# Moving the attention into the first product, and splitting one more half-size product a second time

## The chip, the cores and the metric

The kernel runs on one core of one Trainium2 chip. The metric is device microseconds (us) of one execution; the kernel before takes 954.35 us, the median of three runs that lie between 954.01 and 954.46 us. Everything is 32-bit float.

Engines are named as the profile names them: PE is TensorE, PEld its weight loads, DVE is VectorE, ACT is ScalarE, SPq is the queue of SyncE, from which nearly all transfers are issued.

## The reference

```python
# attention without softmax: batch 8, 8 heads, 576 positions, head size 64
kv  = np.einsum('bhsd,bhse->bhde', k, v)
out = np.einsum('bhsd,bhde->bhse', q, kv)
rms = np.sqrt(np.mean(out * out, axis=-1, keepdims=True) + 1e-06)
x   = (out / rms * g_norm)         # then laid out as 4608 tokens x 512
# feed-forward part, d_model 512, d_ff 2048
h = x @ w_in
r = np.maximum(h, 0.0)
g = s * (r * r) + b
y = g @ w_out
```

## The kernel before: the parts that the change touches

The 4608 tokens are taken in nine units (u = 0 to 8) of 512 tokens. A unit has two stages. The first stage (`mm1`) makes h and g, in four steps s = 0 to 3 of 512 columns of h each. The second stage (`mm2`) makes y. Beside these, the attention of a unit is made in four chunks of 128 tokens; each chunk has four parts: `turn` (DVE transposes q), `product` (16 small matmuls on PE, a square on ACT, a sum on DVE), `norm` (a root on ACT, a reciprocal and a multiply on DVE), and `turn_x` (DVE transposes the result, ACT scales it).

Both large products use a Strassen-Winograd scheme: a 2 x 2 block product is made of seven products of sums of blocks in place of eight. They are numbered 1 to 7 here; the sums on the token side are called S1 to S4, those on the weight side T1 to T4. In the second stage product 5 is S1 T1, product 6 is S2 T2, product 7 is S3 T3, and product 3 has S4. From unit 2 on, products 1, 2, 7 and 4 of the second stage are themselves made by the same scheme ("twice"): seven products of 128 x 128 blocks. A plain product of the seven is 2 x 8 matmuls of 128x256 (`product`, once for each half j of 256 tokens); one made twice is 7 x 4 matmuls of 128x128 (`second_level`, `go`).

```python
TWICE = (1, 2, 7, 4)
ORDER = (1, 2, 6, 7, 5, 3, 4)

def product(i, j, ps, first):          # a plain product, one half j: 8 matmuls of 128x256
    for f in range(FC // 2):
        s, b = divmod(f, 2)
        ...
        matmul(ps, ga[G_OF[i], s][:, b, j * P : j * P + P], w2, first and f == 0, f == FC // 2 - 1)

def scaled(o, ps, other):              # DVE: o = ps * s + other   (line 671 of the profile)
    nc.vector.scalar_tensor_tensor(o, ps, s_col, other, ALU.mult, ALU.add)

def second_level(i, other, to, x_tag="y"):
    def sums(which=(5, 6, 7, 3)):      # four DVE adds or subtractions of 128x512 (lines 230, 233)
        ...
    def go(m, bank, first):            # 4 matmuls of 128x128
        ...
    def keep(name, j, q):
        r[name] = late["tmp"].tile([P, P], FP32, name="r", tag="r")
        scaled(r[name], t["x"], other(j, cols[q]))
    def m1():
        go(1, "x", True)
        keep("r1", 0, 0)               # r1 is read out of bank x ...
    def m2():
        go(2, "z", True)
        scaled(to(0, cols[0]), t["z"], r["r1"])
    def m6():
        go(6, "x", False)              # ... before product 6 is accumulated onto bank x
        keep("r2", 1, 0)
    ...                                # m7 on bank y, m5 and m3 on x, m4 on y
```

So each product made twice asks for four sums ahead (128x512), and for seven small reads of PSUM (128x128). Product m6 adds to the bank that m1 left, and may start only when DVE has read r1 out of it.

The second stage in its order, with the attention of the next unit in between:

```python
            ...                        # product 1 twice; the last of the first stage lies in it
            product_q[0]()             # attention, chunk 0
            p2[1]()
            step["x3_s3"]()
            p2[2](); p2[6]()
            s2((0, 1))
            p2[7](); p2[5]()
            s2((2, 3))
            pump(2)
            norm[0]()
            p7["sums"]()
            x6_of(0)
            p2[3](); p2[4]()
            ...                        # two adds of b_12
            attend(1); turn_x[0](); turn[2]()
            x6_of(1)
            p7[1]()
            s4((0,))
            p7[2](); p7[6]()
            ...                        # attend(2), x5_of(0), p7[3], p7[4], attend(3), x5_of(1), x3, p4
```

(Calls that stood on lines of their own are set side by side here, and `pump` calls are cut in places.) DVE carries out its instructions in this order of the program.

Weights of the second stage come through a ring of seven buffers of 4 KB per partition; `pump(n)` issues the next n loads of a queue, each of which waits on SPq until its buffer is free. k and v have two buffers of their own; q is loaded at the start of a unit for the next one.

```python
late["ring"] = ctx.enter_context(tc.tile_pool(name="ringp", bufs=7, side="right"))
late["sub"]  = ctx.enter_context(tc.tile_pool(name="subp", bufs=5, side="right"))
late["kv"]   = ctx.enter_context(tc.tile_pool(name="kvp", bufs=2, side="right"))
```

Of the kernel before, what the change touches and what calls it, by code (L numbers as in the profile page):

```python
# [16 lines left out]
def kernel(  # L17
# [78 lines left out]
    def load_kv(b, i, pool, queues=(nc.sync, nc.sync), **kw):  # L96

        t = pool.tile([P, 4 * R * D], U32, name="kv_sb", **kw)
        kv_in[b, i] = t.bitcast(FP32).rearrange("p (m l j d) -> p m l j d", m=2, l=2, j=R)
        for m, src in enumerate((k, v)):  # L100
            for r, queue in enumerate(queues):
                h = NP * r + 2 * i
                queue.dma_start(  # L103
                    out=kv_in[b, i][r * HB : r * HB + HB, m].rearrange("p l j d -> p l (j d)"),
                    in_=src[b, h : h + 2].rearrange("h (p j) d -> p h (j d)", j=R),
                )
# [168 lines left out]
    TWICE = (1, 2, 7, 4)  # L275
# [55 lines left out]
    b_12 = const.tile([P, HN], FP32, name="b_12")  # L331

    def bias_row():

        nc.vector.tensor_scalar(out=b_sq, in0=b_sq, scalar1=b_col, scalar2=None, op0=ALU.mult)
        ps = ps_t.tile([P, DM], FP32, name="b_ps", tag="t")
        matmul(ps, b_sq, b_row, True, True)
        nc.scalar.copy(b_row, ps)
        sub(b_12, b_row[:, :HN], b_row[:, HN:])
# [8 lines left out]
    def kv_product(b):  # L348


        ps = [ps_t.tile([P, 2, D], FP32, name="kv_ps", tag="t") for _ in range(2)]
        for i in range(2):
            if b == 0:
                warm((18, 7)[i])
            kv = kv_in.pop((b, i))
            for j in range(R):
                for l in range(2):
                    for r in range(2):
                        rows = slice(r * HB, r * HB + HB)
                        nc.tensor.matmul(  # L360
                            ps[r][l * HB : l * HB + HB, i, :],
                            lhsT=kv[rows, 0, l, j, :],
                            rhs=kv[rows, 1, l, j, :],
                            start=(j == 0),
                            stop=(j == R - 1),
                        )
        for r in range(2):
            for l in range(2):
                ls = slice(l * HB, l * HB + HB)
                to = bd_kv[b % 2][ls, 2 * r : 2 * r + 2, ls].rearrange("p i (c e) -> p i c e", c=KC)  # L370
                src = ps[r][ls].rearrange("p i (e c) -> p i c e", c=KC)
                if b == 0 and l == 1:
                    nc.vector.tensor_copy(out=to, in_=src)
                else:
                    nc.scalar.copy(to, src)

    xT = {}

    def attention(c, first=False):
# [70 lines left out]
        def turn_x():  # L450
            u, j = divmod(c, 4)
            if j == 0:
                xT[u] = xp.tile([P, KC, 2 * TB], FP32, name="xT", tag="xT")
# [175 lines left out]
    late = {}  # L629

    def twice(u, i):
        return u > 1 and i in TWICE

    queue_w2 = [
        (u, i, n) for u in range(1, U) for i in ORDER for n in range(4 if twice(u, i) else 2)
    ]

    def pump(k):

        for u, i, n in queue_w2[:k]:  # L640
            t = late["ring"].tile([P, 4 * HN], FP32, name="w2_sb", tag="w2")
# [14 lines left out]
    def mm2(u, step=None, att=None):  # L656


# [30 lines left out]
        def second_level(i, other, to, x_tag="y"):  # L689
# [23 lines left out]
            def go(m, bank, first):  # L713
                if first:
                    tag = {"x": x_tag}.get(bank, bank)
                    t[bank] = bank_of((bank, i), tag, 1 if tag == "z" else 2)
                    t[bank] = t[bank].rearrange("p b n -> p (b n)")[:, :P]
# [119 lines left out]
        def x3(j):  # L837
            product(3, j, st["x", j], False)
            scaled(rows("o1", j)[:, HN:], st["x", j], b2 if u == 1 else st["o1", j][:, HN:])
# [44 lines left out]
        if u == 1:  # L884
# [5 lines left out]
                lambda: x6(0),  # L890
# [11 lines left out]
        def right(name, j, q=slice(0, HN)):  # L902
            return rows(name, j)[:, HN:][:, q]

        p1 = second_level(1, lambda j, q: b2[:, q], lambda j, q: right("o1", j, q), "x")
        p2 = second_level(2, lambda j, q: right("o1", j, q), lambda j, q: rows("o1", j)[:, q])
        p7 = second_level(
            7, lambda j, q: right("o1", j, q), lambda j, q: right("o2", j, q)
        )
        p4 = second_level(4, lambda j, q: st["r2", j][:, q], lambda j, q: rows("o2", j)[:, q])  # L910

        def x6_of(j):
            st["x", j] = half(("x", j), "x")
            product(6, j, st["x", j], True)
            part("r2", j, st["x", j], b_12)

        def x5_of(j):
            product(5, j, st["x", j], False)

        def with_7(j):  # L920

            to = right("o2", j)
            add(st["r2", j], st["r2", j], to)
            scaled(to, st["x", j], to)
# [10 lines left out]
        turn, product_q, norm, turn_x, x_sums_next = att or [[lambda: None] * 4] * 5  # L935

        def attend(c):
            product_q[c]()
            norm[c]()

        def sums_ahead():
            p1["sums"]()
            turn[0]()
            turn[1]()

        def all_of_it():
# [12 lines left out]
            p1[4]()  # L959
            step["x3_s1"]()  # L960
            pump(2)
            product_q[0]()
            p2[1]()
            step["x3_s3"]()
            p2[2]()
            p2[6]()
            s2((0, 1))
            p2[7]()
            p2[5]()
            s2((2, 3))  # L970
            pump(2)
            norm[0]()
            p7["sums"]()
            x6_of(0)
            p2[3]()
            p2[4]()
            for j in range(2):
                left = rows("o1", j)[:, :HN]
                add(left, left, b_12)
            pump(2)  # L980
            attend(1)
            turn_x[0]()
            turn[2]()
            x6_of(1)
            pump(2)
            p7[1]()
            s4((0,))
            p7[2]()
            p7[6]()
            s4((1,))  # L990
            p7[7]()
            s4((2,))
            p7[5]()
            s4((3,))
            pump(2)
            attend(2)
            turn_x[1]()
            turn[3]()
            x5_of(0)
            p7[3]()  # L1000
            with_7(0)
            p7[4]()
            pump(2)
            attend(3)
            turn_x[2]()
            x5_of(1)
            with_7(1)
            turn_x[3]()
            pump(2)
            p4["sums"]()  # L1010
            x3(0)
            for m in (1, 2, 6, 7, 5):
                p4[m]()
            pump(2)
            x_sums_next[0]()
            x3(1)
            pump(2)
# [4 lines left out]
        return sums_ahead, all_of_it  # L1022
# [4 lines left out]
    def tc_late():  # L1027
        convp.release()
        late["ring"] = ctx.enter_context(tc.tile_pool(name="ringp", bufs=7, side="right"))
        late["sub"] = ctx.enter_context(tc.tile_pool(name="subp", bufs=5, side="right"))  # L1030
        late["tmp"] = ctx.enter_context(tc.tile_pool(name="tmpp", bufs=4, side="right"))
        late["kv"] = ctx.enter_context(tc.tile_pool(name="kvp", bufs=2, side="right"))
# [93 lines left out]

    def side_of(u):

        if u + 1 >= U:
            return None  # L1130
        turn, product, norm, turn_x, _ = zip(*(attention(c) for c in range(4 * u + 4, 4 * u + 8)))
        if u > 1:
            sums = lambda: [sums() for sums in x_sums(u + 1)]
            return turn, product, norm, turn_x, [sums]
# [25 lines left out]

    kv_due = {(b // 2 * R + b % 2 * 4) // 4 - 1: b for b in range(2, B)}

    def loads(u):
        if u + 1 < U:
            load_q(4 * u + 4)
            load_q(4 * u + 6)
# [14 lines left out]

    for u in range(U):
        if u > 0:
            loads(u)
        steps = [mm1(u, s) for s in range(NS)] if u > 0 else []

        def x3(a):
            for name in ("x3", "x3_square", "x3_s1", "x3_s3"):  # L1190
                a[name]()

        def y4(a):
            for name in ("y4", "y4_square"):
                a[name]()

        slots = []
        for s, a in enumerate(steps):
            slots.append(a["x1"])
            if s:  # L1200
                slots.append(partial(x3, steps[s - 1]))
            slots.append(a["z2"])
            if s:
                slots.append(partial(y4, steps[s - 1]))
            slots += [a["x6"], a["y7"], a["x5"]]
        if u == 0:
            first_unit()
        side = side_of(u)
        second = mm2(u, steps[-1], side) if u > 1 else mm2(u)
        for n, slot in enumerate(slots):  # L1210
            slot()
            if u > 1 and n == len(slots) - 2:
                second[0]()
            if u == 1 and n in (1, 3, 5):
                for sums in sums_w_in((n + 1) // 2):
                    sums()
            if u in kv_due and n == 12:
                kv_product(kv_due[u])
            elif u + 1 in kv_due and n == 14:
                for i in range(2):  # L1220
                    load_kv(kv_due[u + 1], i, late["kv"], tag="kv")
        if u > 1:
            second[1]()
            continue
        for n, slot in enumerate(second):
            slot()
            if u == 0:
                if n == 1:
# [3 lines left out]
                    loads(0)  # L1232
# [13 lines left out]
        if u == 0:  # L1246
            tc_late()
            for i in range(2):
                load_kv(kv_due[1], i, late["kv"], tag="kv")
# [31 lines left out]
```

## Time and profile before

| | busy us | share of the span | instructions |
|---|---|---|---|
| span | 954.8 | | 17222 |
| PE | 939.9 | 98% | 7102 |
| DVE | 611.3 | 64% | 1100 |
| ACT | 194.5 | 20% | 366 |

Line 91 is the helper that issues every matmul but those of the attention (line 422) and of k times v (line 360). Lines 230 and 233 are the DVE helpers `add` and `sub`, line 671 is `scaled`, line 569 the copy of a partial result by ACT in the first stage. Lines 155 and 103 load q, and k and v; 645 and 648 are the ring's loads, 772 the stores. The names before and after the arrow are of tiles: `x_ps`, `y_ps`, `z_ps` and `t_ps` are PSUM banks, `sub` are sums, `r` is what `keep` leaves, `o` are rows of the output, `qT` and `xT` the turned q and x.

In the chain of waits a count such as x16 holds both the matmuls and their weight loads: x16 is eight matmuls.

### The profile page before, as it was taken

Reading aid. Unit: us, or ns where it says so; the run is one execution under the profiler, and the core shown is the slowest. Engines: PE = TensorE matmul, PEld = TensorE weight load, DVE = VectorE, ACT = ScalarE, POOL = GpSimd, SP = SyncE. Lnnn points to the kernel's source line nnn. Section 1 sums busy time; section 2 is a strip of 40 time slices with the busy share of each in tenths; the row PEclk is TensorE's granted clock in tenths of the full one; section 3 lists DMA queues with packets and bytes.
Section 4 is the critical chain, followed back from the end, with each engine's and each line's share of the span. In section 5 each row is a group of like instructions: output and inputs, shape, how many; then the busy total and the mean of one; then the engine's idle time right before and its main releaser. Section 6 shows DMA issues by size and latency. Waiting matters only on the chain.

```text
span 954.8 us, 17222 instructions
## 1 busy us (share of the span) xinstructions
PE 939.9 (98%) x7102; PEld 839.9 (88%) x7102; DVE 611.3 (64%) x1100; ACT 194.5 (20%) x366; POOL 6.7 (1%) x18
## 2 busy tenths in 40 slices
PE   6999999999999999999999999999999999999997
PEld 6888888888889998999889988989899989998997
DVE  1779768475447854686368744884478557864673
ACT  2674132211111112111211212121211111111100
POOL 2000000000000000000000000000000000000000
PEclk9999999999999999999999999999999999999999
DMA  9588929587735666365437554566225541662063
GB/s 216 192 310 230 309 69 260 107 249 253 210 69 140 181 189 138 76 201 159 128 81 200 185 159 84 159 197 181 32 81 180 184 87 42 202 176 68 20 223 100
DMA packets 131709, 151.09 MB, mean 158 GB/s; under 512 B 76592, under 2 KB 89136, under 8 KB 131504
## 3 DMA queue, kind: packets, MB, share of 16 engines
q1 hardware_dynamic: 128528, 148.22, 54.1%
q10 hardware_dynamic: 2784, 1.77, 0.8%
q8 instruction: 56, 0.92, 0.4%
q14 instruction: 21, 0.17, 0.1%
q0 software_dynamic: 320, 0.00, 0.0%
HBM read 125.83 MB, written 24.12 MB: 157 GB/s over the span
## 4 chain that ended last, share of the span: by engine, by line
PE 95%; DMA 2%; DVE 1%; ACT 1%; issue 0%; SPq 0%; ACTq 0%; DVEq 0%
PE x_ps L91 49%; PE y_ps L91 32%; PE z_ps L91 9%; PE x_ps L422 3%; PE kv_ps L360 2%; DMA w_raw<-in_moe_w_in_dram 1%; DMA kv_sb<-in_k_dram 1%; PE qT_ps L401 0%; DVE xn L441 0%; DVE xT L465 0%; ACT xT L471 0%; ACT w_raw L210 0%; ACT w_raw L205 0%; SPq L103 0%; DVE wb L225 0%
## 5 line engine op out<-in xcount | busy, mean ns | idle before, releaser
L91 PE MATMUL x_ps<-w_sb,a 128*128 128x256 f32 (+1 forms) x600 | 130.9, 371 | 0.0
L569 ACT COPY r<-x_ps 128x512 f32<-128x512 f32 x96 | 56.2, 585 | 332.4 <-PE x_ps L91 325.6
L91 PEld LDWEIGHTS x_ps<-w_sb,a 128*128 128x128 f32 x600 | 108.6, 190 | 15.2 <-issue 1.6
L91 PE MATMUL y_ps<-xs,wb 128*128 128x256 f32 x512 | 121.0, 379 | 0.0
L91 PE MATMUL x_ps<-xs,ws 128*128 128x256 f32 x512 | 120.9, 379 | 0.0
L230 DVE TENSOR_TENSOR a<-y_ps,r 128x512 f32<-128x512 f32 x64 | 44.1, 688 | 102.1 <-ACT r L569 96.4
L91 PEld LDWEIGHTS x_ps<-xs,ws 128*128 128x128 f32 x512 | 97.3, 190 | 13.2
L91 PEld LDWEIGHTS y_ps<-xs,wb 128*128 128x128 f32 x512 | 96.7, 190 | 12.9
L91 PE MATMUL x_ps<-xT,wa 128*128 128x256 f32 x384 | 89.6, 380 | 0.1
L91 PE MATMUL y_ps<-w_sb,sub 128*128 128x128 f32 x728 | 89.3, 275 | 0.0
L91 PEld LDWEIGHTS y_ps<-w_sb,sub 128*128 128x128 f32 x728 | 86.8, 192 | 1.3 <-DVE r L671 0.2
L91 PEld LDWEIGHTS x_ps<-xT,wa 128*128 128x128 f32 x384 | 72.3, 190 | 10.2 <-ACT xT L471 0.5
L91 PE MATMUL y_ps<-w_sb,a 128*128 128x128 f32 (+1 forms) x472 | 70.0, 294 | 0.0
L524 DVE SCALAR_TENSOR_TENSOR a<-a 128x512 f32<-128x512 f32 x96 | 66.4, 691 | 3.1
L91 PEld LDWEIGHTS y_ps<-w_sb,a 128*128 128x128 f32 x472 | 63.7, 191 | 4.1 <-issue 1.4
L603 DVE TENSOR_TENSOR a<-a 128x512 f32<-128x512 f32 x32 | 22.1, 689 | 61.0 <-ACT a L600 61.0
L91 PE MATMUL x_ps<-xT,ws 128*128 128x256 f32 x256 | 61.1, 382 | 0.0
L91 PE MATMUL z_ps<-xT,wa 128*128 128x256 f32 x256 | 60.5, 379 | 0.0
L91 PE MATMUL x_ps<-w_sb,s 128*128 128x256 f32 x256 | 59.1, 384 | 0.0
L91 PEld LDWEIGHTS x_ps<-w_sb,s 128*128 128x128 f32 x256 | 47.4, 190 | 8.4 <-issue 2.6
L91 PEld LDWEIGHTS z_ps<-xT,wa 128*128 128x128 f32 x256 | 48.6, 190 | 6.6
L91 PEld LDWEIGHTS x_ps<-xT,ws 128*128 128x128 f32 x256 | 47.6, 190 | 6.3
(126 smaller groups left out, 1060.4 us busy)
## 6 DMA issues: line engine op xcount, KB each, us to landing
w_sb<-w SPq DMA_DIRECT2D x140, 512.0 KB, 4.4
kv_sb<-in_k_dram SPq DMA_DIRECT2D x30, 288.0 KB, 4.8
kv_sb<-in_v_dram SPq DMA_DIRECT2D x30, 288.0 KB, 7.3
w_raw<-in_moe_w_in_dram SPq DMA_DIRECT2D x8, 1024.0 KB, 7.9
w_raw<-in_moe_w_out_dram SPq DMA_DIRECT2D x8, 1024.0 KB, 5.2
w_sb<-w SPq DMA_DIRECT2D x28, 256.0 KB, 2.8
out_dram<-o SPq DMA_DIRECT2D x104, 64.0 KB, 1.7
q_sb<-in_q_dram SPq DMA_DIRECT2D x144, 32.0 KB, 2.2
```

The costliest lines, as they stand in the source:

```text
L91: nc.tensor.matmul(o, lhsT=lhsT, rhs=rhs, start=start, stop=stop, skip_group_check=True)
L230: nc.vector.tensor_tensor(out=o, in0=a, in1=b, op=ALU.add)
L360: nc.tensor.matmul(ps[r][l * HB : l * HB + HB, i, :], lhsT=kv[rows, 0, l, j, :], rhs=kv[rows, 1, l, j, :], start=(j == 0), stop=(j == R - 1),)
L422: nc.tensor.matmul(ps[32 * p : 32 * p + 32, w, :], lhsT=st["qT"][:, p, 32 * w : 32 * w + 32], rhs=bd_kv[(b if w < 2 else b1) % 2][:, p, :] ...
L524: nc.vector.scalar_tensor_tensor(t, t, 0.0, t, ALU.max, ALU.mult)
L569: nc.scalar.copy(st[name], src)
L603: nc.vector.tensor_mul(ga["a21", s], ga["a21", s], ga["a21", s])
```

## The change

Three things are done together.

1. Product 6 (S2 T2) of the second stage is made twice from unit 2 on, beside 1, 2, 7 and 4. Product 5 (S1 T1) is moved ahead of it and starts the banks that product 3 is later accumulated onto; product 6 no longer shares them. The aim is to do less matrix work.
2. The attention of the next unit is moved from the second stage into the first stage of the unit (from unit 3 on wholly, in unit 2 half), which leaves DVE more room in the second stage. x then needs a second buffer.
3. k and v go through the ring, which gives their two buffers up: four loads of one pair of heads each stand in the queue ahead of a unit's weights. The ring's buffers grow to 4.5 KB per partition, the pool of sums from five to eight.

```diff
-    TWICE = (1, 2, 7, 4)
+    TWICE = (1, 2, 6, 7, 4)
```
```diff
+    kv_due = {(b // 2 * R + b % 2 * 4) // 4 - 1: b for b in range(2, B)}
+    queue_w2 = []
+    for u in range(1, U):
+        queue_w2 += [(u, "kv", n) for n in range(NP if u in kv_due else 0)]
+        for i in ORDER if u == 1 else (1, 2, 5, 6, 7, 3, 4):
+            queue_w2 += [(u, i, n) for n in range(4 if twice(u, i) else 2)]
```
```diff
-        def x6_of(j):
+        def x5_of(j):
             st["x", j] = half(("x", j), "x")
-            product(6, j, st["x", j], True)
-            part("r2", j, st["x", j], b_12)
-
-        def x5_of(j):
-            product(5, j, st["x", j], False)
+            product(5, j, st["x", j], True)
+            scaled(right("o2", j), st["x", j], b_21)
```
The second stage after the change, from product 2 to product 3 (new order, cut from the diff's plus side; lines joined as above):
```python
            pump(2)
            at(0)                      # at(0) to at(4): attention in unit 2 alone
            p2[1]()
            step["x3_s1"]()
            p2[2](); p2[6]()
            step["x3_s3"]()
            p2[7]()
            s2((0, 1))
            p2[5]()
            pump(2)
            x5_of(0)
            s2((2, 3))
            p6["sums"]((5, 6))
            p2[3](); p2[4]()
            pump(2)
            at(1)
            x5_of(1)
            p6["sums"]((7, 3))
            p7["sums"]((5, 6, 7))
            at(2)
            pump(2)
            p6[1]()
            s4((0,))
            p6[2](); p6[6]()
            s4((1,))
            p6[7](); p6[5]()
            s4((2,))
            pump(2)
            ...
            p7[1](); p6[3](); s4((3,)); p6[4]()
            pump(2)
            p7[2](); p7[6](); p7[7](); p7[5]()
            pump(2)
            at(3)
            x3(0, between)             # between: p7["sums"]((3,)), p4["sums"](), p7[3], p7[4], pump(2), p4[1]
            ...
```
In the first stage the four parts of a chunk are set between the products:
```python
        for s in range(NS):
            j = s if u > 2 else s - 2
            if j >= 0:
                places = [(s, n) for n in range(4)] if s < 3 else [(2, 3), (3, 0), (3, 1), (3, 2)]
                for place, fn in zip(places, (turn, product, norm, turn_x)):
                    first.setdefault(place, []).append(fn[j])
```
The places of step s are: (s, 0) before product 1, (s, 1) after product 2, (s, 2) after product 6, (s, 3) after product 7. The product of k and v stands at (1, 2) in units 1 to 6, with `pump(4)` after it. From unit 3 on, the second half of the next unit's q is loaded at the start of a unit, and the first half one unit earlier still, at (1, 2).

## The prediction

> **What bounds the kernel now.** I read the page's busy times first, then the chain of waits in order of time, then the timeline of DVE and of SPq in one steady unit, and last the list of waits.
>
> ```profile
> PE 939.9 (98%) x7102; PEld 839.9 (88%) x7102; DVE 611.3 (64%) x1100; ACT 194.5 (20%) x366; POOL 6.7 (1%) x18
> ...
> PE 95%; DMA 2%; DVE 1%; ACT 1%; issue 0%; SPq 0%; ACTq 0%; DVEq 0%
> ```
> The chain runs through PE for 95% of the span. PE is the bound, and only what shortens its row of matmuls, or puts a hole into it, counts.
>
> The chain in order of time, inside the second stage of unit 7 (start, length, what):
> ```profile
> 813.72 2.68 PE y_ps L91 x24
> 816.40 3.46 PE x_ps L91 x16
> 819.86 1.78 PE y_ps L91 x16
> 821.64 1.01 PE x_ps L422 x32
> 822.65 3.65 PE x_ps L91 x16
> ```
> x24 is twelve 128x128 matmuls in 2.68 us, 0.2233 us each; x16 of x_ps is eight 128x256 in 3.455 us (neighbouring lines of the same kind read 3.45 and 3.46), 0.4318 us each. A chunk of attention takes 1.01 us and leaves the next group 0.19 us longer (3.65): 1.2 us. So a unit without k and v should be 112 x 0.4318 for the first stage, 48 x 0.4318 for three plain products, 112 x 0.2233 for four products made twice, and 4 x 1.2: 48.4 + 20.7 + 25.0 + 4.8 = 98.9 us. The trace has its units 7 and 8 starting at 755.97 and 854.87, 98.9 us apart. PE has no holes left in a steady unit, and the list of waits says the same:
> ```profile
> PEld y_ps L91 <- DVE r L671: 0.2, 1, 0.2
> ```
> That is all the time that PE waited, in 954.8 us, for DVE to read a partial product out of its bank.
>
> The timeline of DVE, in the same unit (start, length of one, line, operation), at the four sums of product 4 and the first read after them:
> ```profile
> 843.09 0.65 DVE L230 TENSOR_TENSOR sub<-a,a 128x512 f32<-128x512 f32 x1
> 843.77 0.69 DVE L233 TENSOR_TENSOR sub<-sub,a 128x512 f32<-128x512 f32 x1
> 844.38 0.69 DVE L233 TENSOR_TENSOR sub<-a 128x512 f32<-128x512 f32 x1
> 844.98 0.69 DVE L233 TENSOR_TENSOR sub<-a,sub 128x512 f32<-128x512 f32 x1
> 845.59 0.48 DVE L671 SCALAR_TENSOR_TENSOR o<-x_ps,s_col,o 128x256 f32<-128x256 f32 x1
> 846.26 0.35 DVE L671 SCALAR_TENSOR_TENSOR r<-y_ps,s_col,or 128x128 f32<-128x128 f32 x1 [0.19 <-PE y_ps L91]
> ```
> From start to start a 128x512 sum costs DVE 0.61 us, or 0.7 when it needs the one just before; a 128x256 read 0.40 (842.06 to 842.46 elsewhere in this timeline), and a 128x128 read lasts 0.35. A read begins 0.2 us after PE has left the bank: PE ends at 846.06, DVE starts at 846.26.
>
> And SPq at the start of unit 4:
> ```profile
> 453.63 3.86 SPq L772 DMA_DIRECT2D out_dram<-o  x8
> 457.59 0.87 SPq L645 DMA_DIRECT2D w_sb<-w  x2
> 458.51 34.80 SPq L155 DMA_DIRECT2D q_sb<-in_q_dram  x64
> ```
> 64 loads of q take SPq 34.8 us, 0.54 us each. SPq is a queue with long stretches of work, so order there matters too.
>
> [...]
>
> **The change part by part.**
> (a) Product 6 made twice, seven units (2 to 8). It removes 16 matmuls of 128x256 and adds 28 of 128x128 a unit: 16 x 0.4318 = 6.91 against 28 x 0.2233 = 6.25, so 0.66 us less a unit, 4.6 us in all. The order of instructions confirms the counts: 112 fewer of 128x256, 196 more of 128x128. This is all that can be gained, 0.5%, since PE does nothing else less.
> (b) Attention moved: the same 16 small matmuls a chunk, the same 1.2 us of PE, now between products of the first stage. No gain by itself. Per chunk DVE moves turn 0.65, sum 0.69, reciprocal 0.2, multiply 0.69, transpose 0.70: 2.9 us, 11.7 us a unit.
> (c) DVE gains per unit four sums (2.5 us) and seven 128x128 reads, and loses two of 128x256. From unit 7's first matmul of the second stage to its last (800.86 to 854.87) DVE is busy for 42.6 of 54.0 us. After, that stretch loses 10.3 us of attention (two of the turns stood ahead of it) and gains 4 x 0.69 + 7 x 0.35 - 2 x 0.48 = 4.3: 36.6 us of 48.6 (54.0 less 4.8 and 0.66). In sum it is less loaded, 75% against 79%.
> (d) But sums do not decide it; order does. I follow DVE through product 5 and the start of product 6, with zero where PE ends the second half of product 5 (x5_of(1)) and starts p6[1]. PE wants: m1 0 to 0.89, m2 to 1.79, then m6, which adds to the bank that m1 left and needs r1 read. DVE's order in the built program between these is: scaled of product 5, two sums of product 6, three of product 7, then r1. The first of these waits for PE, so it cannot start before 0.2. DVE cannot have run ahead: from the first half of product 5 on it has about 3.5 us of work in PE's 5.2 us (3.46 + two of 0.89), and it stands idle at x5_of(1). From there: 0.2, scaled to 0.60, five sums (four at 0.61, one dependent at 0.7) to 3.74, r1 to 4.09. PE starts m6 about 0.15 us later (weights loaded), at 4.24 in place of 1.79. That is a hole of 2.45 us in each unit. In unit 2 a turn_x and a turn (2 x 0.63) stand before r1 as well: 3.7 us. Sum: 6 x 2.45 + 3.7 = 18.4 us.
> After it DVE catches up: r2 ends 1.35 us after m6 begins, and m5 needs it only after m6 and m7, 1.79 us. I find no second hole in products 6, 7, 3 and 4; the read before p4's m6, which has the same pattern, has the 3.46 us of x3(0) for its five sums.
> (e) Smaller, less sure. In units 3 to 6 the k and v product stands between chunk 1's product and its norm; its four copies on ACT (0.26 each) come ahead of the root, the scaling of xT (four at 0.44) comes later and ahead of the copy r4, on which product 3 of that step waits: about 0.4 us a unit, 1.6. In unit 4 SPq issues 12 more k and v loads ahead of 48 of q, so q for chunks 2 and 3 may come 2 us late. I count half of these: 2 us.
> Sum: -4.6 + 18.4 + 2 = +15.8, or 970.
>
> **The rivals.**
> R1: the hole of (d) does not exist, because DVE is ahead or r1 does not hold m6. Then only (a) remains: 949.8. For it speaks DVE's lower load in (c), and that before had only 0.2 us of such waits. Against it: before has no sums between the read of its plain product and r1 of the next product; there p7's sums stood ahead of x6_of(0).
> R2: the hole also cools PE's clock. [...] if each hole cost a further 1 to 3 us of half speed, 7 x 2 = 14 more: some 984.
> R3: k and v through the ring make loads late, and PE waits for DMA. The ring's order gives p6 and p7 loads 5 us and more from freed buffer to use, against 4.4 us to landing (page, w_sb), so I expect little; a steady 1 us a unit would make 977.
>
> **Range and chances.** The main path gives 970 with about 4 us either way; R1, which I hold at about one in ten, pulls the middle a little lower: 969.5 us, range 960 to 977. Two per cent slower is 973.4: reached if (e) is whole and R2 or R3 adds something, chance 0.2. Two per cent faster is out of reach of (a): 0.02. Within 2%: 0.78.
>
> **What would show it.** In the trace after: the list of waits has t_ps of line 91 waiting for DVE r (the read) some 2.4 us, seven times, longest in unit 2; PE's busy time falls by about 4.6 us while the span grows; units 7 and 8 are 98.2 + 2.45 = 100.7 us apart (98.9 before). DVE shows a run of five 128x512 sums right after the 128x256 read, beside an idle PE. I am wrong if no such wait exists (R1), if the clock in those slices is below 1 (R2), or if PE waits for w_sb (R3).

## The result, and the profile after

| | before | after |
|---|---|---|
| time, median (lowest to highest), 6 runs each | 954.18 us (953.79 to 954.46) | 985.38 us (982.29 to 988.69) |
| ratio | | 1.0328 (95%: 1.0301 to 1.0354) |
| profiled span, granted clock | 954.8 us, 0.997 | 980.5 us, 0.990 |

The changed kernel is 3.3% slower. (The execution of before that was profiled took 956.6 us, 2.4 more than the median of its six timed runs; that of after, 982.29 us, is the fastest of its six.) The line of busy times and the shares of the chain, from the page of the kernel after:
```profile
PE 945.9 (96%) x7270; PEld 846.2 (86%) x7270; DVE 641.9 (65%) x1167; ACT 192.8 (20%) x366; POOL 6.7 (1%) x18
...
PE 87%; DVE 5%; DMA 4%; ACT 2%; SPq 1%; issue 1%; DVEq 0%; ACTq 0%
```
PE's share of the chain fell from 95% to 87%, and DVE's rose from 1% to 5%: the end is now also set by work of DVE. PE's busy time did not fall by the 4.6 us of saved matmuls but rose by 6.0, which is a sign that some matmuls became slower. In these views each matmul of the kernel stands as two MATMUL instructions (the four of m1 are x8 below), and its weight loads stand under PEld: x24 in a line of PE is twelve matmuls. The list of waits (total us, times, longest) says where DVE comes in:
```profile
PEld t_ps L91 <- DVE r L697: 17.8, 7, 3.6
PE t_ps L91 <- DVE r L697: 16.5, 7, 3.4
```
This is the successor of the line with 0.2 us in the profile before: seven waits, one in each unit from 2 to 8, 16.5 us in all. Line 697 is `scaled`, 671 before.

**One hole, in the timeline.** Unit 5 after, PE's groups at m1 and m6 of product 6, and DVE's instructions from the read of product 5 to that of r1 (start, length, what; in brackets the idle time before it and what ended it):
```profile
641.37 1.05 PE L91 MATMUL t_ps<-w_sb,a 128*128 128x128 f32 x8
...
641.58 0.48 DVE L697 SCALAR_TENSOR_TENSOR o<-x_ps,s_col,b 128x256 f32<-128x256 f32 x1 [1.58 <-PE x_ps L91]
641.98 0.68 DVE L245 TENSOR_TENSOR sub<-a 128x512 f32<-128x512 f32 x1
...
642.57 0.69 DVE L245 TENSOR_TENSOR sub<-a,sub 128x512 f32<-128x512 f32 x1
643.18 0.68 DVE L242 TENSOR_TENSOR sub<-a,a 128x512 f32<-128x512 f32 x1
643.89 0.69 DVE L245 TENSOR_TENSOR sub<-sub,a 128x512 f32<-128x512 f32 x1
644.50 0.68 DVE L245 TENSOR_TENSOR sub<-a 128x512 f32<-128x512 f32 x1
645.11 0.34 DVE L697 SCALAR_TENSOR_TENSOR r<-t_ps,s_col,o 128x128 f32<-128x128 f32 x1
...
645.50 4.57 PE L91 MATMUL t_ps<-w_sb,sub 128*128 128x128 f32 x24 [2.18 <-DVE r L697]
```
DVE stood idle for 1.58 us until PE left the bank of product 5 (641.58). Then it read that bank, made five sums of 128x512, and only at 645.11 read r1, for which PE had been ready since about 643.3. PE starts 0.39 us after that read began. The read at 641.58 is the one that PE's own work holds back, and everything behind it in DVE's order is late by the five sums.

**What follows the hole.** The last line has a second number to look at: 4.57 us for twelve 128x128 matmuls. In the profile before, such a group took 2.68 us in the chain. The same kernel's windows show why (stretch, length, then busy time and count of PE, PEld, DVE, ACT, POOL, then the granted clock, DMA share and GB/s), unit 5 above and unit 4 below the gap:
```profile
643.00:645.40 2.40, 0.32 (x3) 0.13 (x2) 2.37 (x6) 0.00 (x0) 0.00 (x0) 1.00 0.91 332
645.50:646.50 1.00, 1.00 (x7) 1.00 (x8) 0.81 (x2) 0.00 (x0) 0.00 (x0) 0.78 0.22 82
646.50:647.50 1.00, 1.00 (x6) 1.00 (x6) 0.36 (x2) 0.00 (x0) 0.00 (x0) 0.50 0.00 0
647.50:648.50 1.00, 1.00 (x7) 1.00 (x6) 0.59 (x1) 0.00 (x0) 0.00 (x0) 0.50 0.00 0
648.50:649.50 1.00, 1.00 (x7) 1.00 (x7) 0.00 (x0) 0.00 (x0) 0.00 (x0) 0.52 0.07 16
649.50:650.50 1.00, 1.00 (x11) 1.00 (x11) 0.35 (x2) 0.00 (x0) 0.00 (x0) 1.00 0.50 152
...
539.20:541.60 2.40, 0.33 (x3) 0.13 (x2) 2.37 (x6) 0.00 (x0) 0.00 (x0) 1.00 0.84 276
541.70:542.70 1.00, 0.99 (x8) 0.99 (x9) 0.81 (x2) 0.00 (x0) 0.00 (x0) 1.00 0.40 148
542.70:543.70 1.00, 1.00 (x11) 1.00 (x10) 0.79 (x2) 0.00 (x0) 0.00 (x0) 1.00 0.00 0
```
In unit 5 the clock falls to 0.50 about half a microsecond after PE resumes and stays there for about 3.4 us (0.44 + 1 + 1 + 0.96, from the means of the four stretches); PE is busy all the time but has 6 or 7 matmul instructions in a microsecond in place of 11. The three products m6, m7, m5 take 4.57 us against 2.94 where the clock holds: 1.63 us lost beside the hole itself. Unit 4 has the same hole to 0.01 us, and its clock holds. In this trace five of the seven holes cool the clock, that is, halve it (units 2, 3, 5, 6, 7); two do not (4, 8).

**Two smaller waits in the first stage.** From the timeline of the kernel after, chunk 0 of attention in unit 2 and chunk 2 in unit 4:
```profile
307.66 1.08 PE L434 MATMUL x_ps<-bd_kv,qT 128*32 128x128 f32 x32 [1.58 <-DVE qT L404]
...
492.54 0.71 DVE L404 STREAM_TRANSPOSE qT<-q_sb 128x512 f32<-128x512 f32 x1 [3.80 <-DMA q_sb<-in_q_dram]
...
493.39 1.08 PE L434 MATMUL x_ps<-bd_kv,qT 128*32 128x128 f32 x32 [2.34 <-DVE qT L404]
```
In unit 4 the turn waits for the transfer of q, and PE for the turn. In unit 2 it is DVE that has other work ahead of the turn.

**The balance, unit by unit.** The times from one unit's first matmul to the next one's, read from PE's timeline in both traces:

| unit | before | after | difference | of which |
|---|---|---|---|---|
| start to unit 1 | 144.66 | 141.03 | -3.63 | first weights landed earlier |
| 1 | 104.51 | 105.18 | +0.67 | |
| 2 | 101.36 | 107.85 | +6.49 | hole 3.6, clock 1.6, turn of q 1.6, saved -0.66 |
| 3, 5, 6 | 101.36 | 105.43 | +4.07 each | hole 2.45, clock 1.63, first stage 0.67, saved -0.66 |
| 4 | 101.36 | 106.20 | +4.84 | hole 2.45, first stage 3.07 (q 2.34), saved -0.66 |
| 7 | 98.90 | 102.34 | +3.44 | hole 2.45, clock 1.63, saved -0.66 |
| 8, to the end | | | +1.69 | hole 2.45, saved -0.66 |

("Hole" is what a unit takes longer for it: the idle 2.18 us, 0.17 us by which a group otherwise begins before the one ahead of it ends (m1 and m2 last 1.06 us and start 0.89 apart), and 0.10 us in the group behind it, 2.94 us for 2.84 without a hole. As a whole: 103.80 us in a unit with the hole at full clock, unit 3 of the same kernel run again, against 101.35 without it, both below.) The start is hardly the change's: 3.56 us of its difference are there by 30 us, where PE's instructions are still the same in both, and so are the transfers sent up to 24 us. Before waits longer there for its first weights; in after the same wait is 1.35 us:
```profile
24.48 0.63 PE L459 MATMUL xT_ps<-ident,xn 128*128 128x128 f32 x4 [3.75 <-ACT w_raw L210]
```
From 25.0 to 28.4 us, behind this wait, the granted clock of before is 0.50. The first unit began between 140.4 and 142.5 us in the other kernels below, so 144.66 was late. Without the start the units add 29.3 us: holes 18.3, clock 8.2 (5 x 1.63), unit 4's first stage 3.1, that of units 3, 5 and 6 2.0, unit 2's attention 1.9, unit 1 0.7, and 4.6 saved come to 29.5.

### The profile page after: what moved, and what is told of

It reads as the page before. It is cut to its first block, busy times and chain, and to the rows that moved or that the text cites. A ratio compares the mean times of both kernels' runs of the same rounds, so it can differ in the third digit from the quotient of the medians.

```text
span 980.5 us, 17772 instructions
## 1 busy us (share of the span) xinstructions
PE 945.9 (96%) x7270; PEld 846.2 (86%) x7270; DVE 641.9 (65%) x1167; ACT 192.8 (20%) x366; POOL 6.7 (1%) x18
## 4 chain that ended last, share of the span: by engine, by line
PE 87%; DVE 5%; DMA 4%; ACT 2%; SPq 1%; issue 1%; DVEq 0%; ACTq 0%
PE x_ps L91 39%; PE y_ps L91 26%; PE z_ps L91 9%; PE t_ps L91 8%; PE x_ps L434 3%; DVE sub L245 2%; PE kv_ps L372 2%; DMA w_sb<-w 1%; SPq L167 1%; DMA w_raw<-in_moe_w_in_dram 1%; DMA kv_sb<-in_k_dram 1%; ACT xT L484 1%; DVE o L697 1%; DVE sub L242 0%; DVE xT L478 0%
## 5 line engine op out<-in xcount | busy, mean ns | idle before, releaser
L91 PE MATMUL x_ps<-w_sb,a 128*128 128x256 f32 (+1 forms) x376 | 79.7, 364 | 0.0
L91 PE MATMUL t_ps<-w_sb,sub 128*128 128x128 f32 x448 | 63.1, 302 | 16.5 <-DVE r L697 16.5
L91 PEld LDWEIGHTS t_ps<-w_sb,sub 128*128 128x128 f32 x448 | 60.4, 215 | 18.2 <-DVE r L697 17.8
L91 PEld LDWEIGHTS x_ps<-w_sb,a 128*128 128x128 f32 x376 | 66.9, 190 | 8.4 <-issue 0.6
L91 PE MATMUL y_ps<-w_sb,sub 128*128 128x128 f32 x504 | 62.0, 275 | 0.0
L91 PEld LDWEIGHTS y_ps<-w_sb,sub 128*128 128x128 f32 x504 | 60.2, 192 | 0.7
L91 PE MATMUL y_ps<-w_sb,a 128*128 128x128 f32 (+1 forms) x360 | 54.3, 300 | 0.0
```

Of the source, the lines that this page charges most:

```text
L91: nc.tensor.matmul(o, lhsT=lhsT, rhs=rhs, start=start, stop=stop, skip_group_check=True)
```

## The experiments

The theory after the trace: (A) the five sums ahead of r1 make the holes, and (B) the holes halve the clock, which costs 1.63 us each time; (C) attention in the first stage adds the rest. Rivals: that the slow matmuls come from something else that begins there (transfers, bank t), not from idle time; that the second level of product 6 is itself more dear than counted; and that the attention would be free if the sums were placed better.

### Sums ahead of what holds them

e1_sums_early is the kernel after with the five sums ahead of the two halves of product 5, in whose 3.5 us DVE has room:
```diff
+            p7["sums"]((5, 6, 7))
             x5_of(0)
             ...
             at(1)
+            p6["sums"]((7, 3))
             x5_of(1)
-            p6["sums"]((7, 3))
-            p7["sums"]((5, 6, 7))
```


> The kernel after, with the three sums of product 7 set ahead of the first half of product 5's read and the sums 7 and 3 of product 6 ahead of the second half's. Theory A (the order of DVE's queue makes the hole, the hole makes the slow clock): both go, 16.5 us of waits and about 8 us of half clock, so about 956 us; waits of t_ps for r under 1.5 us in all, PE clock 0.997, units 3, 5 and 6 at 101.4 us. Rival B (DVE has too much work in the second stage, the hole only moves): another wait of several us takes its place, time above 968.

Measured: 962.13 us (958.64 to 962.88), ratio to before 1.0086 (1.0062 to 1.0109). The same place in its unit 5, from the timeline:
```profile
636.25 0.48 DVE L697 SCALAR_TENSOR_TENSOR o<-x_ps,s_col,b 128x256 f32<-128x256 f32 x1 [0.38 <-PE x_ps L91]
637.14 0.35 DVE L697 SCALAR_TENSOR_TENSOR r<-t_ps,s_col,o 128x128 f32<-128x128 f32 x1 [0.41 <-PE t_ps L91]
...
637.84 2.84 PE L91 MATMUL t_ps<-w_sb,sub 128*128 128x128 f32 x24
```
The read of r1 now waits for PE, no longer PE for it, and m6 follows without a gap. Units 3, 5 and 6 take 101.35, 101.35 and 101.34 us and unit 7 98.26: against after, 4.1 us less in each, which is hole and clock together. Only the order of five DVE instructions was touched, so (A) is shown; the one hole left is of 0.60 us, in unit 2. The whole is 6 us longer than expected, and nearly all of it is unit 4, with 107.84 us:
```profile
488.00 1.94 PE L434 MATMUL x_ps<-bd_kv,qT 128*32 128x128 f32 x32 [3.90 <-DVE qT L404]
489.86 3.67 PE L91 MATMUL y_ps<-xs,wb 128*128 128x256 f32 x8
```
PE reaches the chunk earlier now, so it waits longer for the same q, 3.90 us in place of 2.34, and the clock halves behind it (1.94 for the chunk that otherwise takes 1.08, 3.67 for the four 128x256 that otherwise take 1.99).

### Half of it

e2_half moves the two sums of product 6 alone:
```diff
             at(1)
+            p6["sums"]((7, 3))
             x5_of(1)
-            p6["sums"]((7, 3))
             p7["sums"]((5, 6, 7))
```


> Only the sums 7 and 3 of product 6 are moved ahead, the three of product 7 stay behind product 5. Theory A: the hole shrinks by two sums, 1.2 us, to about 1.0 us a unit, and if a hole that short leaves the clock alone the time is 980 - 8.4 - 8.2 = 964 us. If every hole cools the clock whatever its length (rival C), it is 972 us and the clock in the slices of product 6 still reads 0.5 in most units.

Measured: 970.70 us (969.93 to 972.15), ratio 1.0188 (1.0172 to 1.0203). Unit 5, timeline:
```profile
643.42 0.34 DVE L697 SCALAR_TENSOR_TENSOR r<-t_ps,s_col,o 128x128 f32<-128x128 f32 x1
...
643.82 2.94 PE L91 MATMUL t_ps<-w_sb,sub 128*128 128x128 f32 x24 [0.98 <-DVE r L697]
```
Three sums make a hole of 0.98 us where five made 2.18: 1.2 us for two sums, as their 0.61 us each says. The group behind it takes 2.94 us in all six units, so none of these holes cools the clock; units 3, 5 and 6 take 102.60 us. The time as a whole would have suited the rival (972), but the units do not: the excess is unit 4 again, 110.19 us, with a wait for q of 4.87 us and a halved clock after it (the chunk takes 1.93 us in place of 1.08). The total alone would mislead here.

### The hole filled, not removed

e3_fill keeps the order of after and gives PE ten 128x128 matmuls of the identity to do between m2 and m6, into a bank that the attention leaves idle there. Their result is not read; it is added work:
```diff
             p6[2]()
+            ps = ps_a.tile([P, NP, P], FP32, name="x_ps", tag="x")
+            for _ in range(10):
+                matmul(ps[:, 0, :], ident, ident, True, True)
             p6[6]()
```


> The kernel after with ten matmuls of 128x128 into an unused bank (2.23 us, result not read) between m2 and m6 of product 6, where PE sat idle. If idle PE is what halves the clock: the wait for r shrinks to 0.2 us, product 6's m6 to m5 take 2.7 us in all units, clock 0.997, and the time falls by the clock's part alone, to 972 us. If the slow matmuls have another cause (PSUM bank, ring, DVE traffic): time stays at 981 to 988 us.

Measured: 977.57 us (974.75 to 980.06), ratio 1.0257 (1.0232 to 1.0282). Timeline, unit 5:
```profile
640.49 2.40 PE L91 MATMUL x_ps<-ident 128*128 128x128 f32 x20
642.84 2.94 PE L91 MATMUL t_ps<-w_sb,sub 128*128 128x128 f32 x24
```
The late read of r1 is the same and the same time passes until m6, but PE is not idle, and the group behind takes 2.94 us. Units 3, 5 and 6 take 103.81, 103.80 and 103.80 us (after 105.43): 1.63 us less, by adding work. This settles (B): the slow matmuls come from PE's idle time, not from the transfers or the bank, which are unchanged. The medians fall by 7.8 us (985.38 to 977.57), near the 8.2 of the clock; the 972 that was expected was counted from 980, the span of the fastest execution. Unit 7 takes 100.71 us.

### Without the second level of product 6

e4_plain6 keeps attention and k, v as in after, and makes product 6 plain on bank t (products 1, 2, 7 and 4 twice, as before the change). Nothing is left out:
```diff
-    TWICE = (1, 2, 6, 7, 4)
+    TWICE = (1, 2, 7, 4)
+        def x6_of(j):
+            ps = ps_t.tile([P, DM], FP32, name="t_ps", tag="t")[:, :HN]
+            product(6, j, ps, True)
+            s4((2 * j, 2 * j + 1))
+            scaled(right("o1", j), ps, right("o1", j))
```


> The kernel after with product 6 left plain (two halves of eight 128x256 matmuls into bank t), attention, k and v, and product 5 first as after. Theory A: no hole, so it shows the rest of the change alone: 0.66 us more a unit than e1, that is 956 + 4.6 = 960 to 961 us, 6 us above before, from the first stage (0.7 us a unit in units 3 to 6), q in unit 4 (2.3) and the turn in unit 2 (1.6). If moving the attention were free it would be 954; if making product 6 twice were the whole loss it would be 954 too.

Measured: 964.03 us (961.59 to 965.60), ratio 1.0114 (1.0095 to 1.0132). Units 3, 5 and 6 take 102.01, 101.99 and 102.00 us and unit 7 98.92. Against e1 (101.35 and 98.26) that is 0.64 to 0.66 us: the saving of product 6 twice is what the count of matmuls says. (Units 2 and 8 don't show it so: e1 has its hole of 0.60 us in unit 2, and from unit 8 to the end e4 takes 0.46 us more.) Against before (101.36 and 98.90) units 3, 5 and 6 lose 0.65 us and unit 7, whose first stage holds only attention and no k and v, nothing. Unit 4 takes 108.81 us (q late by 4.18), unit 2 103.28. So the rest of the change (attention moved, k and v through the ring, product 5 ahead) costs some 11 us by itself, most of it in unit 4, and saves nothing.

### q a unit earlier

e5_q is e1 with the second half of q, from that of unit 5 on, sent to its buffers at (2, 3) of the unit before, once the chunks that lay in them have been turned:
```diff
+        if u > 2:
+            first[2, 3].append(lambda: loads(u + 2, 1))
...
-            loads(u + 1, 0 if u < 3 else 1)
+            if u < 4:
+                loads(u + 1, 0 if u < 3 else 1)
```


> The kernel with the sums set early, and from unit 4 on the second half of q loaded a unit earlier (at step 2 of the first stage, behind the turn of chunk 3). Theory A: unit 4's extra 6.5 us (107.8 against 101.3) is q, held up on SPq behind 12 k and v loads and 8 stores, and the cold clock after that wait; it goes, units 3 to 6 are then alike at 101.3 to 101.4, and the time is 962.1 - 6.5 = 955.6 us. Rival: the loads of q at their new place hold up the ring's loads, and PE waits for w_sb early in the second stage; then other units grow by 1 us or more each.

Measured: 956.55 us (955.31 to 957.72), ratio 1.0039 (1.0025 to 1.0054). Unit 4 takes 101.36 us in place of 107.84. Unit 3 takes 102.87, 1.5 us more, for a reason that the timeline names:
```profile
417.56 3.69 PE L91 MATMUL x_ps<-w_sb,s 128*128 128x256 f32 x16 [1.29 <-DMA w_sb<-w]
```
The loads of q now stand ahead of a weight load in SPq's order, and PE waits 1.29 us for that. It is the prediction's rival R3, called forth by the cure.

### The rest of the first stage

e6_all is e5 with four places changed: `norm` ahead of the product of k and v at (1, 2); unit 2's turn of chunk 2 earlier, at (3, 3) of its first stage; also in unit 2, `at(2)` (a `turn_x` and a `turn`) behind `p6[5]` in place of ahead of `p6[1]`; and, in unit 1, weight sums one call later. Cut:
```diff
-                seq(lambda: x6(0), lambda: parts_of_w(6)),
-                seq(lambda: x6(1), lambda: pump(2)),
+                lambda: x6(0),
+                seq(lambda: x6(1), lambda: parts_of_w(6), lambda: pump(2)),
...
-                    first.setdefault(place, []).append(fn[j])
+                    at_place = first.setdefault(place, [])
+                    at_place.insert(0 if fn is norm else len(at_place), fn[j])
...
+            first.setdefault((3, 3), []).append(turn[2])
```


> As e5_q, and with the three small waits taken out: the norm ahead of the k and v product (units 3 to 6, 0.5 us each), in unit 2 the turn of chunk 2 a stage earlier (1.6) and the turn_x and turn behind product 6 (0.6), in unit 1 the sums of w for product 6 one half later (0.5). Theory A: 955.6 - 2.0 - 2.2 - 0.5 = 951 us, 2 to 3 us under before, ratio 0.997 to 0.998; units 3 to 6 at 100.8. If 28 products of 128x128 were not worth the 0.66 us a unit they should save, it stays at 955 or above.

Measured: 953.77 us (952.11 to 957.16), ratio 1.0010 (0.9999 to 1.0020). Units 4, 5 and 6 take 100.95, 100.95 and 100.94 us: of the 0.67 us by which the first stage had grown, 0.40 go with the place of `norm`. Unit 2 takes 101.46 (103.46 in e1). Unit 1 was made worse, 105.51, so that step missed; unit 3 still pays for q (102.40). The time is 2.8 us over the 951 expected.

### A shorter hole

e7_fill3 is e3 with three matmuls in place of ten, so that a hole of some 1.5 us is left; again their result is not read:
```diff
             p6[2]()
+            ps = ps_a.tile([P, NP, P], FP32, name="x_ps", tag="x")
+            for _ in range(3):
+                matmul(ps[:, 0, :], ident, ident, True, True)
             p6[6]()
```

> The kernel after with three dummy matmuls of 128x128 (0.67 us) in the hole in place of ten, so that PE stands idle for about 1.5 us in units 3 to 8. The unit's length stays (the end of the hole is set by DVE). [...] (holes of 1.0 us cooled it in none, 2.2 us in four of six); if any hole over 1 us does it, five or six.

Measured: 980.91 us (one run). Timeline, the groups after the holes of units 2 and 3:
```profile
328.23 4.58 PE L91 MATMUL t_ps<-w_sb,sub 128*128 128x128 f32 x24 [2.70 <-DVE r L697]
...
434.85 2.94 PE L91 MATMUL t_ps<-w_sb,sub 128*128 128x128 f32 x24 [1.52 <-DVE r L697]
```
All six holes of 1.5 us leave the clock alone (2.94 or 2.95 us for the group behind); unit 2's, 2.70 us long, does not (4.58).

### The version with all cures

e8_best is e6 with unit 1 as in after but its turn of chunk 1 one place earlier, and with the last 16 of the 48 loads of q for unit 5 held back until unit 4 starts:
```diff
-            3: [product[0]],
-            4: [turn[1]],
+            3: [product[0], turn[1]],
...
-            first[2, 3].append(lambda: loads(u + 2, 1))
+            first[2, 3].append(lambda: loads(u + 2, 1, 1 if u == 3 else 0))
```


> As e6_all, but the last 16 of the 48 loads of q that unit 5 needs are sent at the start of unit 4 in place of ahead of unit 3's ring loads, and in unit 1 the turn of chunk 1 stands one product earlier, ahead of the sums of w for product 6 (which go back to their place). Theory A: unit 3 falls from 102.4 to 101.0 us (its wait of 1.2 us for w_sb goes) and unit 1 from 105.5 to 104.9; the time is 953.8 - 2.0 = 951.8 us, 1.5 to 2 us under before, ratio 0.998. If the loads of q only collide elsewhere, unit 4 grows by 1 us or more and the ratio stays at 1.001.

Measured: 950.74 us (950.15 to 951.98), before on the same chip 953.13, ratio 0.9976 (0.9966 to 0.9986): under before by 0.24%, and faster than after. From its page:
```profile
PE 936.9 (99%) x7270; PEld 839.8 (88%) x7270; DVE 642.7 (68%) x1167; ACT 192.4 (20%) x366; POOL 6.7 (1%) x18
```
The same 7270 matmul instructions as after take 9.0 us less of PE's time, PE is busy for 99% of the span, and from unit 1 on PE has no wait of 0.6 us or more. Units 3 to 6 take 100.95 us (before 101.36) and unit 7 98.26 (98.90). The change as a whole now gains 2.4 us, where product 6 alone was to bring 4.6: the first stage of units 3 to 6 still takes 52.42 us, 0.27 more than the 47.35 of before and four chunks of 1.2.

### The changed kernel once more

e9_after_again is the kernel after, unchanged, to see whether the same holes cool.

> The kernel after, unchanged, once more. Theory A: the holes are fixed by the order of instructions, so they come again with the same lengths (2.2 us in six units, 3.4 in unit 2); [...] If the slow matmuls came from the instruction order too, the same five units (2, 3, 5, 6, 7) would be slow again.

Measured: 984.63 us (one run). From its timeline, units 3 and 5, and the chunk of unit 4 between them:
```profile
434.08 2.94 PE L91 MATMUL t_ps<-w_sb,sub 128*128 128x128 f32 x24 [2.19 <-DVE r L697]
...
494.05 1.56 PE L434 MATMUL x_ps<-bd_kv,qT 128*32 128x128 f32 x32 [4.10 <-DVE qT L404]
495.55 3.15 PE L91 MATMUL y_ps<-xs,wb 128*128 128x256 f32 x8
...
647.85 4.57 PE L91 MATMUL t_ps<-w_sb,sub 128*128 128x128 f32 x24 [2.19 <-DVE r L697]
```
The holes have the same lengths, but other units cool: 2, 5, 6 and 7, and no longer 3, which takes 103.80 us. q came later (4.10 against 2.34 us), and that cooled the clock too. So the order fixes the holes, but not what they cost further: the times of after spread over 6.4 us in six runs, those of before over 0.7. In the trace of after, a hole cooled the clock where 2.05 to 2.19 us of it lay in one step of 3.413 us, and did not where it was split into 0.71 and 1.47 or 1.25 and 0.93 (last section).

## Why the prediction was wrong

- Step (a), product 6: 0.66 us a unit. Shown, by e4 against e1, 0.64 to 0.66 us in units 3, 5, 6 and 7.
- Step (b), attention neutral for PE: right where it stands alone (first stage of unit 7: 44.89 before, 49.73 after, 4.84 for four chunks).
- Step (c) was right that DVE's load is not what counts (64% before, 65% after), and step (d) right in mechanism and in size: 2.45 us predicted, 2.45 measured (2.18 of it idle); 3.7 predicted in unit 2, 3.6 measured. e1 shows it. That the first two agree to the hundredth is luck: in unit 5 m6 starts 4.13 us after m1, not 4.24, and the group behind is 0.10 us longer, which the prediction did not count. R1, a missing hole, is refuted.
- **The step that failed is R2's dismissal.** The prediction had the right rival, with a cost (1 to 3 us each, some 984 us in all) and the sign to look for, and left it out of its sum, even for the longer hole in unit 2. That holes of this length leave the clock alone was not shown: beside the 3.75 us wait at the start, with a clock of 0.50 behind it, PE has no wait over 0.93 us between matmuls in the trace of before, so no hole of such a length stood there to measure by, and the range should have reached R2's own number, 984. In after, holes of 2.18 us halved the clock in four of six units, that of 3.37 in unit 2 as well, 8.2 us in all (e3 shows that it is the idle time). The length alone does not tell which: the same 2.18 us left the clock at 1.00 in units 4 and 8 (last section).
- Step (e) was halved without a reason, and it too was short. It put the first stage of units 3 to 6 at 0.4 us each (measured 0.67) and q in unit 4 at 2 us (2.34), together 3.6, and counted 2; the measured 2.0 in units 3, 5 and 6 and 3.1 in unit 4 make 5.1. Unit 2's 1.9 us, where the turn of q stands behind sums, and 0.7 in unit 1 were not in the list.
- R3, weights late through the ring, did not appear in after. It appeared in e5, when q was put ahead of them.

In sum: predicted +15.8 before weighing. The holes came as counted (18.3 for 18.4), the clock adds 8.2, and (e) with units 1 and 2 adds 5.6 over what was counted: 29.5, less 3.6 for the late start in the one trace of before gives 25.9, against 25.7 between the two spans. (The medians lie 31.2 apart: the profiled run of after is 3.1 us under its median, that of before 2.4 over its own.)

## What to carry to other kernels

Before adding instructions to an engine that is not the bound, list its queue between each read that the bound waits for and the last thing that engine itself waits for. What stood between held the bound up here, though DVE was busy for only 65% of the span: five sums made a hole of 2.18 us. Such sums belong ahead of the wait, not behind it. A hole in a stream of matmuls can be dearer than its length: here by 1.63 us in 7 of 12 holes of 2.18 to 2.19 us, and in none of the 23 waits of 0.98 to 1.59 us. And when a cure moves one wait away, look at once for the transfer that it puts behind another.

## What the runs showed of the hardware

The length of PE's idle time against the clock after it, for all waits of 0.9 us and more from unit 1 on in the eleven traces (in before and in e8 there is none). For after the clock was read from the trace, for the others it is told by the matmuls behind the wait: where it is halved, a group of twelve takes 4.37 to 4.58 us in place of 2.94, and a chunk of attention 1.56 to 1.94 in place of 1.08.

| idle us | places | clock halved |
|---|---|---|
| 0.98 to 1.29 | holes in e2 (6) and e3, weights in e5 and e6 | 0 of 9 |
| 1.51 to 1.59 | holes in e7 (6), turn of q in unit 2 (8 kernels) | 0 of 14 |
| 2.18 to 2.19 | holes in after (6) and the same again (6) | 7 of 12 |
| 2.34 to 2.70 | q in after and e3, unit 2's hole in e2 and e7 | 1 of 4 |
| 3.37 | unit 2's hole in after and the same again | 2 of 2 |
| 3.48 to 4.87 | q in e1, e2, e4, e7 and after again | 5 of 5 |

Length alone does not sort these cases. In the trace of after the falls of the clock behind waits are at 328.61, 434.43, 646.05, 751.87 and 854.27 us, which are 31, 62, 31 and 30 times 3.413 us apart, and each slow stretch behind them is 3.413 us long. Counted in steps of this length from those falls, PE's idle time in after is:

| wait in after | steps from (us) | PE idle in the step, us | clock in the next step |
|---|---|---|---|
| hole of unit 2, 3.37 us | 321.79 and 325.20 | 1.32 and 2.05 | 1.00 and 0.50 |
| holes of units 3, 5, 6 and 7, 2.18 to 2.19 us | 431.01, 642.64, 748.45, 850.85 | 2.18 or 2.19 | 0.50 |
| hole of unit 4, 2.18 us | 536.82 and 540.24 | 0.71 and 1.47 | 1.00 |
| hole of unit 8, 2.18 us | 946.43 and 949.84 | 1.25 and 0.93 | 1.00 |
| q in unit 4, 2.34 us | 489.04 and 492.45 | 1.39 and 0.94 | 1.00 |
| turn of q in unit 2, 1.58 us | 304.72 | 1.58 | 1.00 |

So the 2.18 us of unit 5's hole lie in one step, 642.64 to 646.05 us, while unit 4's are split. In before, PE is idle for 2.86 us from 21.61 to 25.02 us, and the clock is 0.50 from there to 28.44. That is what these two traces show; what the hardware counts is not shown, nor a limit for other work.

A slow stretch costs 1.63 us where these matmuls fill all of it: 4.57 us for 2.94 behind holes of 2.18 us, and behind the 3.37 us of unit 2 the same group with the four matmuls after it 5.30 us, for 3.67 in unit 4.
